# Units of 512 tokens that begin at a batch's start, and the batches' ends as a last unit

## The chip, the cores and the metric

The kernel runs on one core of a Trainium2 chip. Its time is the device time of one execution in microseconds (us), the median of three runs. The profile is one more execution with the hardware profiler on.

## The reference

Three parts follow one another. The first is attention within chunks of 64 tokens, the second a mixture of experts that sends each token to at most one expert, the third a layer with the largest of three products.

```python
# q, k, v: (8, 8, 576, 64) batch, head, token, dim; chunk = 64
scores = scale * np.matmul(q_c, k_c.transpose(0, 1, 2, 4, 3))
attn = softmax(scores)                      # within the chunk
out = np.matmul(attn, v_c)
x = out.transpose(0, 2, 1, 3).reshape(4608, 512)
do = x @ w_skip > 0                         # the rest pass unchanged
e = argmax(x @ w_gate); gate = softmax(x @ w_gate)[e]
x[do] += gate * (relu(x @ w1[e]) @ w2[e])
return max(x @ m1, x @ m2, x @ m3) @ w_out  # 768 wide, then 512
```

The chunks of 64 divide 576 evenly, and nothing in the parts after the attention depends on the order of the tokens. The weights of the third part are held in 64-bit floats.

## The kernel before

The 4608 tokens are 36 tiles of 128, in the order of batch and token. Three stages follow one another, and all of x goes through device memory (`x_dram`) between them.

**Attention and routing** (lines 124 to 683). `values`, `scores`, `exp_transpose`, `logits`, `qk_transpose` and `x_transpose` are the work of PE, and the loop at line 610 gives them their order by hand: step t takes the values of tile t-2, the scores of tile t, the turned exponentials of tile t-1, the logits of tile t-3, the turning of one job of q and k, and the turned rows of tile t-2. The order on the other engines is made by a planner from modelled times.

q and k come in 18 units (`load_qk`, line 195). Units 0 and 1 are 256 tokens with all heads, two tokens to a partition (512 B runs). Units 2 to 17 are 512 tokens with four of the eight heads, four tokens to a partition (1 KB runs), and two of them, with the same tokens, make what `item_of` numbers U (2 to 9). `pieces(t, end)` (line 182) cuts a range of tokens where a batch of 576 ends, and each piece is one load for q and one for k, on the Sync queue (line 214). The ranges of U = 2 to 8 each hold one such end: U = 2 is 64 tokens of batch 0 on 16 partitions and 448 of batch 1 on 112, the next is 32 and 96 partitions, and so on; U = 9 lies in batch 7. Units 0 and 1 lie in batch 0. That makes 66 loads of q and k.

v comes in tiles of 128 tokens (`load_v`, line 219), 256 B runs, in a ring of eight buffers; the load for tile t+6 is issued in step t. Tiles 4, 13, 22 and 31 hold a batch's end and take two loads of 64 partitions. q and k may run five units ahead of the regrouping.

POOL then copies: `cross` (line 224) puts halves of v on the other partitions, `pair_heads` (line 232) regroups q and k, and `store_x` (line 471) writes four tiles of x to `x_dram`; a tile buffer `xg` is used again two groups later. `send_id` (line 451) scatters each token's number to its expert's list, by rank. After 24 tiles the list of expert 0 is filled up to 256, so that its first two tiles can begin early. From step 22 on the weights of expert 0 are loaded and split (lines 630 to 637).

**Experts** (to line 1020): each of the eight takes its rows in tiles of 128, gathered from `x_dram`, with as many tiles as its count of rows wants, and puts them back.

**The last part** (lines 1024 to 1132): five blocks of rows of `x_dram`; its products leave through `os`, two buffers, copied in turn by VectorE and ScalarE (lines 1127 and 1129), and each tile of 128 rows is stored by one DMA (line 1131). The last block is the last 512 rows in two halves of 256, that is the last four tiles, and its four stores end the kernel.

Of the kernel before, what the change touches and what calls it, by code (L numbers as in the profile page):

```python
# [19 lines left out]
P = 128  # L20
B, H, S, D = 8, 8, 576, 64
# [7 lines left out]
NI = N // UT  # L29
WIDE = 2  # L30
NT = N // P
XW = DM + 8
COLS = NT
SLOTS = E * COLS
# [4 lines left out]
def kernel(  # L39
# [15 lines left out]
    nc = tc.nc  # L55
# [4 lines left out]
    dram = ctx.enter_context(tc.tile_pool(name="dram", bufs=1, space=DRAM))  # L60
    x_dram = dram.tile([N + 1, XW], F32, name="x_dram")
    ids_dram = dram.tile([P * SLOTS, 1], I32, name="ids_dram")
# [9 lines left out]
    def four_kb(shape, dt, name, aside=False):  # L72
        return bpool.tile(shape, dt, tag="s4" if aside else "b4", name=name, bufs=2 if aside else 4)
# [5 lines left out]
    def ps_mm(name):  # L79
        return ps(next(turns["mm"]), name)  # L80
# [8 lines left out]
    def split(src, hi, lo, eng):  # L89
        return (  # L90
            nc.scalar.copy(hi, src),  # L91
            eng.tensor_tensor(lo, src, hi.bitcast(F32), op=ALU.subtract),  # L92
        )
# [35 lines left out]
    for i in range(11):  # L129
# [6 lines left out]
        out=upper_b, in_=upper_b, compare_op=ALU.is_gt, fill=0.0, base=0,  # L136
# [4 lines left out]
    GT = 4  # L141
    SIZES = [GT] * (NT // GT - 1) + [2, 2]
    DIRECT, FIRST = NT - 4, 5
    START = [sum(SIZES[:g]) for g in range(len(SIZES))]
    PLACE = [(g, j) for g, n in enumerate(SIZES) for j in range(n)]
    prio = kpool.tile([P, GT, E], F32, name="prio")
    for e in range(E):
        nc.vector.memset(prio[:, :, e], float(E - e))
    tok_i = cpool.tile([P, NT], I32, name="tok_i")
    nc.gpsimd.iota(tok_i, pattern=[[P, NT]], base=0, channel_multiplier=1)  # L150
    tok_f = kpool.tile([P, NT], F32, name="tok_f")
    col_i = kpool.tile([P, P], I32, name="col_i")
# [23 lines left out]
    for i, t in enumerate(v_all):  # L176
        (nc.gpsimd if i > 1 else nc.vector).memset(t[:, :, D], 1.0)
    none = kpool.tile([1, XW], F32, name="none")
    nc.gpsimd.memset(none, 0.0)
    nc.gpsimd.dma_start(x_dram[N:N + 1, :], none)  # L180

    def pieces(t, end):
        got, t0 = [], t
        while t < end:
            b, s = divmod(t, S)
            n = min(end - t, S - s)
            got.append((t - t0, b, s, n))
            t += n
        return got

# [3 lines left out]
    def item_of(i):  # L194
        return (i, None) if i < WIDE else (WIDE + (i - WIDE) // 2, i % 2)

    def load_qk(i):
        if i % 5 < 3:
            qt = four_kb([P, 1024], F32, f"qt{i}", i % 5 == 2)
            kt = four_kb([P, 1024], F32, f"kt{i}", i % 5 == 2)  # L200
        else:
            both = bpool.tile([P, 2, 1024], F32, tag="b8", name=f"qkt{i}")
            qt, kt = both[:, 0], both[:, 1]
        U, g = item_of(i)
        if g is None:
            r, t0, heads = 2, i * UT, [(0, 4), (4, 8)] if i == 0 else [(0, 8)]
        else:
            r, t0, heads = 4, WIDE * UT + (U - WIDE) * 2 * UT, [(4 * g, 4 * g + 4)]
        for h0, h1 in heads:
            for off, b, s, n in pieces(t0, t0 + P * r):  # L210
                pr = slice(off // r, (off + n) // r)
                for dst, src in ((qt, q), (kt, k)):
                    to = dst[pr].rearrange("p (h x) -> p h x", x=r * D)
                    link["load"] = nc.sync.dma_start(
                        to[:, h0:h1] if g is None else to,
                        src[b, h0:h1, s:s + n, :].rearrange("h (p r) d -> p h (r d)", r=r))
        units[i] = {"qt": qt, "kt": kt}
# [86 lines left out]
    def values(t):  # L304
# [10 lines left out]
        if j == 0:  # L315
            if g == len(SIZES) - 1:
                parts = [four_kb([P, 1, XW], F32, f"xg{g}_{i}", True) for i in range(SIZES[g])]
            else:
                parts = [bpool.tile([P, GT, XW], F32, tag="xg", name=f"xg{g}")[:, :SIZES[g], :]]
            groups[g] = parts, apool.tile([P, GT, E + 1], F32, tag="lg", name=f"lg{g}")  # L320
# [147 lines left out]
    def load_ids(dst, src, eng=nc.sync):  # L468
        follow(eng.dma_start(dst, src), sent, "slots are written in any order")
# [107 lines left out]
    vm, turned, units, xt, groups, slots, picks, xgs, xT, link, put, sent = {}, {}, {}, {}, {}, {}, {}, {}, {}, {}, {}, []  # L577
# [32 lines left out]
    for t in range(NT + LAG):  # L610
        u, s = divmod(t, 2)
        while items and items[0] - 5 <= regrouped:
            load_qk(items.pop(0))
# [36 lines left out]
        if 0 <= t - 4 < NT:  # L650
            g, j = PLACE[t - 4]
            if j + 1 == SIZES[g]:
# [10 lines left out]
                if g == FIRST:  # L663
                    fill_first(run[(g + 1) % 2][:, 0, 0:1])
                    load_ids(ids_0[:, :2], ids_rows[:, :2])
                    xgs[0] = [four_kb([P, XW], F32, f"xg_0_{j}") for j in range(2)]
                    rows = START[g + 1] * P
                    at = cpool.tile([P, 2], I32, name="at")
# [131 lines left out]
    def tiles_of(rows):  # L800
        return [rows[:, j, :] for j in range(4)]

    def gather_tiles(e, js):
        if e not in xgs:
            if e < 2:
                held_rows[e] = bpool.tile([P, 4, XW], F32, tag="xg", name=f"xg_{e}")
            xgs[e] = tiles_of(held_rows[e % 2])
# [31 lines left out]
    def load_block(b, after=()):  # L839
        r0, n = BLOCKS[b]  # L840
        if b not in xin:
            tiles = [bpool.tile([P, 4, XW], F32, tag="xg", name=f"x_{b}_0")]
            if b == 0:
                tiles += [wpool.tile([P, 2, DM], F32, tag="w", name=f"x_0_{i}") for i in (1, 2)]
            elif n == G:
                tiles.append(bpool.tile([P, 4, XW], F32, tag="xg", name=f"x_{b}_1"))
            xin[b] = [t[:, i, :DM] for t in tiles for i in range(t.shape[1])]
        for i, row in enumerate(xin[b]):
            r = r0 + i * P
            follow(nc.sync.dma_start(row, x_dram[r:r + P, :DM]), after, "rows are written in any order")  # L850
# [20 lines left out]
    def ring_ahead(b, unit, by):  # L871
        while wanted and len(ring) < len(SEATS) * (b * len(UNITS) + unit) + by:
            ring_load(wpool if wanted[0][0] == LAST and len(ring) % 11 < 7 else wpool2)
# [45 lines left out]
    rows = bpool.tile([P, 4, XW], F32, tag="xg", name="xg_0")  # L919
# [165 lines left out]
    for b, (r0, n) in enumerate(BLOCKS):  # L1085
        if b < LAST:
            load_block(b + 1)
        hT = {}
        for f in range(NS):
            best = []  # L1090
            for m in range(3):
                ring_ahead(b, 3 * f + m, 8 if b < LAST else 15)
                unit(b, (m, f), best, [aside.pop(0)] if b == 0 and aside else ())
                if b == 0 and 3 * f + m >= 6:
                    for _ in range(min(2, len(rest))):
                        rest.pop(0)()
            for i in (0, 1, 3, 2):
                kf, half = 2 * f + 1 - i // 2, i % 2
                if f < 1:
                    both = four_kb([P, 2, G], F32R, f"fh_{b}_{kf}_{half}")  # L1100
                elif f < 2:
                    if i in (0, 3):
                        two = bpool.tile([P, 2, 2, G], F32R, tag="b8", name=f"fh_{b}_{kf}_{half}")
                    both = two[:, 0 if i in (0, 3) else 1]
                elif i in (0, 1):
                    both = four_kb([P, 2, G], F32R, f"fh_{b}_{kf}_{half}", True)
                else:
                    both = wpool.tile([P, 2, G], F32R, tag="w", name=f"fh_{b}_{kf}_{half}")
                hi, lo = both[:, 0, :n], both[:, 1, :n]
                split(best[i], hi, lo, nc.gpsimd)  # L1110
                hT[kf, half] = hi, lo
        if b < LAST:
            for cc in range(2):
                sums_room(b + 1, cc)
                sums_T(b + 1, cc)
            ring_ahead(b + 1, 0, 4 if b + 1 < LAST else 11)
        for half in range(2):
            for i in range(n // P):
                acc = ps_mm(f"o_{b}_{half}_{i}")
                sl = slice(i * P, (i + 1) * P)  # L1120
                for at, kf in enumerate((1, 0, 3, 2, 5, 4)):
                    hi, lo = hT[kf, half]
                    bhi, blo = mw[3, kf // 2]
                    mm3(acc, hi[:, sl], lo[:, sl], bhi[:, kf % 2, :], blo[:, kf % 2, :], at == 0, at == 5)
                o = fpool.tile([P, DM], F32, tag="o", name=f"os_{b}_{half}_{i}", bufs=2)
                if i % 2:
                    nc.scalar.copy(o, acc)
                else:
                    nc.vector.tensor_copy(o, acc)
                r = r0 + half * n + i * P  # L1130
                nc.sync.dma_start(out[r:r + P, :], o)
    p3.close()


# [28 lines left out]
```

## Time and profile before

| | |
|---|---|
| median of 3 runs | 1152.9 us (1152.66 to 1156.75) |
| the profiled execution | 1149.06 us, its span 1147.3 us |
| PE busy | 1045.2 us, 91% of the span |
| VectorE (DVE), ScalarE (ACT), POOL busy | 574.1, 440.6, 369.7 us |
| moved by DMA | 217.13 MB, 189 GB/s in the mean |
| loads and stores on the hardware queue of Sync (q1) | 183680 packets, 174.18 MB |

A busy PE is one with matmuls in flight, not one at its peak. The DMA share is the mean busy share of 16 DMA engines; a packet counts from its start to its end, so that packets in flight together can bring it above 1. "issue" as a reason for a wait is time in which the engine waited for nothing that the profile shows. A wait for several things is put down to the one that came last.

### The profile page before, as it was taken

What the parts mean: (1) busy time and instruction counts of PE and PEld (TensorE: products, weight loads), DVE (VectorE), ACT (ScalarE), POOL (GpSimd) and SP (SyncE); (2) the same over time, 40 slices, a digit from 0 to 9 for tenths busy, and PEclk for the clock granted to TensorE, in tenths of its full rate; (3) what the DMA queues carried; (4) which work ended last, traced back from release to release, by engine and by line L of the source; (5) the groups of instructions that cost most, each with busy time, mean ns of one, the idle gap of its engine ahead of it and who ended that gap; (6) DMA issues with size and microseconds to landing.
All of it is one profiled execution on the core that took longest, in us unless ns stands there. A gap on an engine that the chain in (4) does not pass through costs nothing.

```text
span 1147.3 us, 19676 instructions
## 1 busy us (share of the span) xinstructions
PE 1045.2 (91%) x7544; PEld 887.4 (77%) x7544; DVE 574.1 (50%) x1118; ACT 440.6 (38%) x737; POOL 369.7 (32%) x411
## 2 busy tenths in 40 slices
PE   7777877887989997999799799999999999999997
PEld 6667767785877877888678678878887888778896
DVE  4545555657784728643359882344423451334241
ACT  5645666423443424442234343222322232222231
POOL 3444465336432415432233323121401231122121
PEclk9978888778989999999999989999999999999999
DMA  9999955237675637742789854665456645666591
GB/s 208 204 225 185 234 141 162 94 114 241 202 281 193 180 117 258 241 170 82 251 273 308 275 167 157 192 188 170 156 149 190 189 131 159 185 187 197 179 299 37
DMA packets 196977, 217.13 MB, mean 189 GB/s; under 512 B 48523, under 2 KB 161163, under 8 KB 196864
## 3 DMA queue, kind: packets, MB, share of 16 engines
q1 hardware_dynamic: 183680, 174.18, 53.6%
q0 software_dynamic: 10592, 33.20, 8.4%
q10 hardware_dynamic: 2592, 8.26, 1.9%
q8 instruction: 69, 1.13, 0.4%
q14 instruction: 44, 0.36, 0.1%
HBM read 175.15 MB, written 41.83 MB: 189 GB/s over the span
## 4 chain that ended last, share of the span: by engine, by line
PE 39%; DMA 6%; DVE 3%; issue 3%; POOL 1%; ACT 0%; SPq 0%; POOLq 0%; DVEq 0%; ACTq 0%
PE f_a L720 5%; PE f_a L722 5%; PE f_a L721 5%; PE o L720 4%; PE o L722 4%; PE o L721 4%; DMA ws<-m_sums 3%; PE f_d L720 3%; PE f_d L722 2%; PE f_d L721 2%; DMA m_sums<-n_q 2%; PE f_b L722 1%; PE f_b L720 1%; PE f_b L721 1%; PE trf L894 1%
## 5 line engine op out<-in xcount | busy, mean ns | idle before, releaser
L92 POOL TENSOR_TENSOR fh<-best,fh 128x512 fp32r<-128x512 f32 (+1 forms) x60 | 77.4, 1295 | 360.5 <-ACT fh L91 275.5
L720 PE MATMUL f_a<-x_t,ws 128*128 128x512 f32 (+1 forms) x270 | 100.9, 374 | 6.0 <-DVE p L1048 5.2
L721 PE MATMUL f_a<-x_t,ws 128*128 128x512 f32 (+1 forms) x270 | 99.9, 370 | 0.0
L722 PE MATMUL f_a<-x_t,ws 128*128 128x512 f32 (+1 forms) x270 | 99.8, 370 | 0.0
L91 ACT CAST whi_e<-raw_e 128x1024 fp32r<-128x1024 f32 x64 | 65.9, 1048 | 62.3 <-DMA raw_e<-in_moe_w_dram 28.5
L720 PE MATMUL h<-xhi,whi_e 128*128 128x256 f32 x256 | 75.3, 295 | 13.3 <-ACTq L997 7.6
L721 PE MATMUL o<-wlo_m,fh 128*128 128x512 f32 x216 | 84.6, 392 | 0.0
L720 PE MATMUL o<-whi_m,fh 128*128 128x512 f32 x216 | 83.4, 392 | 0.0
L722 PE MATMUL o<-whi_m,fh 128*128 128x512 f32 x216 | 83.4, 392 | 0.0
L722 PE MATMUL y<-whi_e,hlo 128*128 128x512 f32 x184 | 73.3, 402 | 3.5 <-DVE hlo L727 3.3
L720 PE MATMUL y<-whi_e,hhi 128*128 128x512 f32 x184 | 74.0, 404 | 0.6 <-ACT hhi L787 0.6
L721 PE MATMUL h<-xlo,whi_e 128*128 128x256 f32 x256 | 74.2, 290 | 0.0
L722 PE MATMUL h<-xhi,wlo_e 128*128 128x256 f32 x256 | 74.0, 290 | 0.0
L721 PE MATMUL y<-wlo_e,hhi 128*128 128x512 f32 x184 | 72.7, 397 | 0.0
L92 DVE TENSOR_TENSOR wlo_e<-raw_e,whi_e 128x1024 fp32r<-128x1024 f32 x43 | 58.5, 1375 | 24.6 <-ACT whi_e L91 21.9
L92 POOL TENSOR_TENSOR wlo_e<-raw_e,whi_e 128x1024 fp32r<-128x1024 f32 x21 | 53.2, 2537 | 51.3 <-ACT whi_e L91 51.1
L91 ACT CAST fh<-best 128x512 fp32r<-128x512 f32 (+1 forms) x60 | 34.7, 579 | 89.6 <-DVE best L1050 57.6
L720 PEld LDWEIGHTS h<-xhi,whi_e 128*128 128x128 f32 x256 | 51.1, 200 | 16.2 <-ACTq L997 8.0
L720 PEld LDWEIGHTS f_a<-x_t,ws 128*128 128x128 f32 x270 | 51.2, 189 | 15.7 <-DVE p L1048 5.7
L1053 ACT COPY p<-f_a 128x512 f32<-128x512 f32 (+1 forms) x45 | 24.5, 544 | 100.5 <-PE f_a L722 100.3
L711 POOL DMA_INDIRECT x_dram<-xg,ids_sb x20 | 21.9, 1096 | 118.5 <-DVEq L935 46.8
L722 PEld LDWEIGHTS f_a<-x_t,ws 128*128 128x128 f32 x270 | 51.2, 190 | 8.7
(220 smaller groups left out, 2759.9 us busy)
## 6 DMA issues: line engine op xcount, KB each, us to landing
ws<-m_sums SPq DMA_DIRECT2D x135, 512.0 KB
raw_e<-in_moe_w_dram SPq DMA_DIRECT2D x64, 512.0 KB
ws<-m_sums SPq DMA_DIRECT2D x45, 256.0 KB
x<-x_dram SPq DMA_DIRECT2D x36, 256.0 KB
out_dram<-os SPq DMA_DIRECT2D x36, 256.0 KB
x_dram<-xg POOLq DMA_DIRECT2D x8, 1040.0 KB
v_all<-in_v_dram SPq DMA_DIRECT2D x32, 256.0 KB
m_sums<-n_raw ACTq DMA_DIRECT2D x18, 448.0 KB
```

The source lines that it names most:

```text
L91: nc.scalar.copy(hi, src),
L92: eng.tensor_tensor(lo, src, hi.bitcast(F32), op=ALU.subtract),
L711: ins = nc.gpsimd.indirect_dma_start(out=x_dram[:, :], out_offset=bass.IndirectOffsetOnAxis(ap=ids, axis=0), in_=xg, in_offset=None, bound ...
L720: nc.tensor.matmul(acc, ahi, bhi, start=first, stop=False, skip_group_check=onto)
L721: nc.tensor.matmul(acc, ahi, blo, start=False, stop=False, skip_group_check=onto)
L722: return nc.tensor.matmul(acc, alo, bhi, start=False, stop=last, skip_group_check=onto)
L894: nc.tensor.transpose(tr[:, i * P:(i + 1) * P], row[:, c * P:(c + 1) * P], ident)
L1053: nc.scalar.copy(p1, acc_a)
```

## The change

The first 512 tokens of the eight batches are put first, batch by batch (4096 tokens, 32 tiles), and the last 64 of each follow as the last 512 (4 tiles). `pieces` returns the parts of a range in that order. So the units U = 2 to 8 are batches 1 to 7, one piece over 128 partitions each, and tiles 0 to 31 of v are one load each. U = 9 is the ends of all batches: its q and k are loaded head by head, eight batches to a load, 16 partitions for each batch, 16 loads in all. Tiles 32 to 35 hold two batches' ends each, so v takes two loads for each. At the end, rows that belong to those tiles are stored by two DMAs of 64 rows to the places of their batches; other tiles by one. `x_dram` and the lists of the experts hold the tokens in the new order. Nothing else changes.

```diff
--- before.py
+++ after.py
@@ -29,6 +29,9 @@
 NI = N // UT
 WIDE = 2
 NT = N // P
+WHOLE = S // P * P
+TAIL = S - WHOLE
+FULL = B * WHOLE // P
 XW = DM + 8
 COLS = NT
 SLOTS = E * COLS
@@ -182,9 +185,9 @@
     def pieces(t, end):
         got, t0 = [], t
         while t < end:
-            b, s = divmod(t, S)
-            n = min(end - t, S - s)
-            got.append((t - t0, b, s, n))
+            b, s = divmod(t, WHOLE) if t < P * FULL else divmod(t - P * FULL, TAIL)
+            n = min(end - t, (WHOLE if t < P * FULL else TAIL) - s)
+            got.append((t - t0, b, s if t < P * FULL else s + WHOLE, n))
             t += n
         return got
 
@@ -206,7 +209,14 @@
             r, t0, heads = 2, i * UT, [(0, 4), (4, 8)] if i == 0 else [(0, 8)]
         else:
             r, t0, heads = 4, WIDE * UT + (U - WIDE) * 2 * UT, [(4 * g, 4 * g + 4)]
-        for h0, h1 in heads:
+        if t0 >= P * FULL:
+            b0, nb = (t0 - P * FULL) // TAIL, P * r // TAIL
+            for h in range(heads[0][0], heads[0][1]):
+                for dst, src in ((qt, q), (kt, k)):
+                    link["load"] = nc.sync.dma_start(
+                        dst.rearrange("p (h x) -> p h x", x=r * D)[:, h - heads[0][0], :],
+                        src[b0:b0 + nb, h, WHOLE:, :].rearrange("b (p r) d -> b p (r d)", r=r))
+        for h0, h1 in heads if t0 < P * FULL else ():
             for off, b, s, n in pieces(t0, t0 + P * r):
                 pr = slice(off // r, (off + n) // r)
                 for dst, src in ((qt, q), (kt, k)):
@@ -1128,7 +1138,9 @@
                 else:
                     nc.vector.tensor_copy(o, acc)
                 r = r0 + half * n + i * P
-                nc.sync.dma_start(out[r:r + P, :], o)
+                for off, b_out, s_out, rows in pieces(r, r + P):
+                    at = b_out * S + s_out
+                    nc.sync.dma_start(out[at:at + rows, :], o[off:off + rows])
     p3.close()
```

## Rows read from the trace of the kernel before

**Rows 1.** Page, part 2: PE, its granted clock, DMA, GB/s in 40 slices.

```profile
PE   7777877887989997999799799999999999999997
PEclk9978888778989999999999989999999999999999
DMA  9999955237675637742789854665456645666591
GB/s 208 204 225 185 234 141 162 94 114 241 202 281 193 180 117 258 241 170 82 251 273 308 275 167 157 192 188 170 156 149 190 189 131 159 185 187 197 179 299 37
```

**Rows 2.** Windows of four tiles: length, busy us (instructions) by engine, clock, DMA share, GB/s.

```profile
20.30:42.40 22.10, 18.33 (x372) 15.67 (x367) 9.37 (x20) 16.89 (x26) 8.54 (x18) 1.00 1.08 205
42.40:66.80 24.40, 18.41 (x356) 16.72 (x357) 13.78 (x43) 16.03 (x27) 8.79 (x18) 0.93 1.18 224
66.80:95.20 28.40, 21.11 (x355) 19.15 (x355) 12.98 (x42) 14.83 (x25) 12.78 (x23) 0.76 1.21 225
95.20:121.00 25.80, 19.52 (x360) 17.71 (x359) 12.88 (x43) 14.55 (x25) 12.68 (x23) 0.87 0.94 186
121.00:148.40 27.40, 22.38 (x351) 19.76 (x350) 12.55 (x42) 15.01 (x26) 17.29 (x28) 0.79 0.84 196
148.40:170.60 22.20, 19.59 (x356) 17.34 (x356) 14.69 (x43) 14.56 (x25) 13.66 (x23) 0.87 0.48 145
170.60:196.80 26.20, 21.20 (x355) 18.67 (x355) 15.76 (x50) 15.40 (x27) 17.39 (x28) 0.80 0.54 168
196.80:221.70 24.90, 20.34 (x338) 17.95 (x338) 14.89 (x44) 14.76 (x26) 10.81 (x19) 0.74 0.31 104
```

**Rows 3.** Windows by kind of load, same columns.

```profile
4.00:10.00 6.00, 4.69 (x26) 3.13 (x28) 0.98 (x2) 3.40 (x6) 1.24 (x4) 1.00 1.01 288
...
64.00:88.00 24.00, 16.71 (x266) 15.46 (x262) 10.69 (x37) 10.06 (x18) 13.35 (x23) 0.72 1.21 210
...
132.00:143.00 11.00, 10.92 (x186) 10.23 (x185) 5.93 (x16) 7.35 (x13) 5.77 (x13) 0.77 1.10 327
```

**Rows 4.** Waits of PE, 42.4 to 148.4 us: total, times, longest.

```profile
PE sc L278 <- issue: 12.4, 18, 3.0
PE trq L262 <- POOL qr L239: 5.7, 2, 3.5
...
PE xp L311 <- issue: 1.4, 1, 1.4
```

**Rows 5.** Waits of PE, 148.4 to 221.7 us.

```profile
PE sc L278 <- issue: 1.6, 3, 0.9
```

**Rows 6.** Waits of POOL, 42.4 to 148.4 us.

```profile
POOL xg L322 <- DMA x_dram<-xg: 26.9, 4, 7.6
POOL vm L230 <- DMA ids_dram<-tok_i,rslot: 12.5, 3, 6.3
```

**Rows 7.** Waits of POOL, 148.4 to 221.7 us.

```profile
POOL xg L322 <- DMA x_dram<-xg: 10.2, 3, 4.1
```

**Rows 8.** Timeline of PE: start, length, idle before in brackets, its releaser.

```profile
36.33 0.66 PE L262 MATMUL trk<-ident,kr 128*128 128x128 f32 x4 [1.14 <-POOL kr L239]
...
49.90 0.29 PE L278 MATMUL sc<-kT,qT 64*64 64x64 f32 x4 [2.95 <-issue]
...
65.77 0.27 PE L311 MATMUL xp<-vm,aT 64*64 64x65 f32 x1 [1.36 <-issue]
...
80.46 1.11 PE L262 MATMUL trq<-ident,qr 128*128 128x128 f32 x4 [3.54 <-POOL qr L239]
...
148.60 0.26 PE L278 MATMUL sc<-kT,qT 64*64 64x64 f32 x1 [0.94 <-issue]
```

**Rows 9.** Tile qt, issues on the Sync queue: ns least/median/most, first and last start.

```profile
L214 SPq DMA_DIRECT2D qt<-in_q_dram x21: 390/663/3767, 0.8 to 134.4; - x21
```

**Rows 10.** Chain that ended last, 1135 us to the end: start, length.

```profile
1140.48 0.34 SPq L1131
...
1140.91 2.28 DMA out_dram<-os
```

## Prediction

> **What bounds the kernel now.** I read the page's slices first. The DMA line stands at 9 for the first five slices (some 143 us) while TensorE (PE) is at 7 or 8 and the granted clock falls below full from the third slice on [rows 1]. This is the attention stage, 36 tiles of 128 tokens, and the only stage whose loads the change touches; the expert stage and the last stage do the same work on the same number of rows afterwards.
>
> So I cut that stage into windows of four tiles, from one normalising multiply (line 326) to the fourth after it [rows 2]. Nothing is steadily full: PE is busy for about three quarters of each window, with its order fixed by hand, so a tile's time is set by whichever helper comes late. The windows between 42.4 and 148.4 us take 24.4, 28.4, 25.8 and 27.4 us, 106.0 together, with a DMA share of 0.84 to 1.21. The next three take 22.2, 26.2 and 24.9 us, 73.3 together, with a share of 0.31 to 0.54. I treat these as the same work with and without busy DMA, though the later ones also cast expert 0's weights (lines 630 to 637).
>
> Then I asked whether the loads or the amount of data make DMA busy [rows 3]. At 4 to 10 us every load covers 128 partitions, in 512 B packets: 288 GB/s at a share of 1.01. At 132 to 143 us the last unit's loads, again 128 partitions and 1 KB packets, run beside v and the store of x: 327 GB/s at 1.10. In between, where a 512-token unit straddles a batch's end and comes as two pieces (16 and 112 partitions, 32 and 96, ...), the same share and more (1.21 at 64 to 88 us) moves 210 GB/s. The engines are as busy and deliver a third less.
>
> Last, I asked who pays. PE waited 12.4 us at the scores and 1.4 at the values for "issue", that is for nothing a semaphore shows, and 5.7 us for GpSimd (POOL) regrouping q: 19.5 us in the four windows [rows 4]. In the three later ones the "issue" wait at the scores is 1.6 us [rows 5]. POOL itself waited 26.9 us for stores of x and 12.5 us before copies of v halves [rows 6]; the second is put down to the id scatter, but the copies that follow it read v, and v loads queue behind q and k, so I read it as late v. In the later windows the store wait is 10.2 us [rows 7]. The longest single gaps are 3.54 us at 80.46 for POOL and 2.95 us at 49.90 for "issue" [rows 8]. [...]
>
> **The change, part by part.** *q and k.* The packets do not change: they were 1 KB and stay 1 KB, and bytes are equal. What goes is the cut. Seven of the eight 512-token units lose it, so the 66 q and k loads become 50 (6 for batch 0, 28 for batches 1 to 7, 16 for the ends). The 28.3 MB of q, k and v take 28.3/0.21 = 135 us at the rate of the cut loads and 87 to 98 us at 327 or 288 GB/s. The windows of [rows 2], 32 of the 36 tiles, reach to 221.7 us, so DMA goes from the thing that is late to a thing with room. What that is worth I bound from both sides by [rows 2]: if the four congested windows run like the mean of the three later ones (24.4 us), they take 97.7 and the gain is 8.3 us; if like the best one (22.2), 88.8 and 17.2 us. The waits agree with the lower end: 19.5 us of PE waits become about 4/3 of 1.6, but the later windows have other waits in their place. I take 12 us, near the middle, since the later windows carry those casts and the earlier ones don't.
>
> *The first tiles.* Up to 42.4 us two heads' groups are turned per step and ScalarE is busy for 16.9 of 22.1 us [rows 2]; the only PE wait here behind a load is 1.14 us at 36.33, for POOL's copy of k [rows 8]. I take 1 us; the bounds are 0 and 3.
>
> *v.* 40 loads before and after. Four split tiles become whole and the last four are split instead, with the same two pieces of 64 partitions; their time is inside the rates above. Cost nothing on their own: tile t's load is issued six steps ahead, some 6 x 6 = 36 us of cover.
>
> *The batches' ends.* Unit 9 now takes 16 loads of 128 KB instead of 4 of 512 KB. They go through the Sync queue, with v loads behind them. One issue takes 0.39 us unhindered, 0.66 in the median and 3.77 at most [rows 9]; 16 are 6 to 11 us, against a lead of 36 us of v and more for q and k. I count them as hidden. [...]
>
> [...]
>
> *The order of tokens.* Rows of x now stand in another order, and routing places them by rank. Worked out from the reference's inputs, each expert's total is the same; expert 0 has 182 instead of 184 rows in the first 24 tiles, which are padded to 256 either way, and 93 instead of 91 after, still one tile. No branch changes. Zero.
>
> *Outputs.* The last block's four stores become eight, of 64 rows. At the end two copies wait for the buffers of two earlier stores: store issue 0.34 us, landing 2.28 us [rows 10]. Each buffer's second store is issued 0.34 us later; the second buffer's comes fourth instead of second, and the last tile has one more issue behind it. That is 0.34 x 2 for the wait and 0.34 for the last store, 1.0 us; if half-size stores land earlier, 0.4. I take +0.9. Elsewhere the store is unchanged.
>
> **The sum.** -12 - 1 + 0.9 = -12.1 us. The profiled execution took 1149.06 us, 1.8 around its span; it would take 1137. The median of the runs is 1152.9, 3.8 above it; taken off there: 1140.8, which I put at 1141. By the bounds: 1133 to 1146. A measurement of this kernel can tell about 0.5%, 5.8 us, from no change.
>
> **Rivals.** *Less comes off.* The "issue" waits may need only a burst of loads, not slow ones. For: around 145 us, right after loads at 327 GB/s, PE still waited, the last time 0.94 us at 148.60 [rows 3, 8]. Against: after 148.4 they nearly vanish [rows 5]. Then only POOL's waits go: 5.7 + 1 - 0.9 = 5.8 us, 1147; if new waits on ScalarE and VectorE fill part of it, up to 1152. Chance 0.21.
>
> *More comes off.* [...] The window at 42.4 has clock 0.93 and took 24.4 us with 2.95 and 1.36 us of gaps in it [rows 2, 8]; without them 20.1, four times 80.4, a gain of 25.6 us: 1127. Against: the window with the least DMA, share 0.31, still took 24.9 at clock 0.74. Chance 0.13.
>
> *Slower: the 16 end loads block the Sync queue.* If each issue takes as long as the longest before (3.77 us) [rows 9], 16 take 60 us, v is 60 - 36 = 24 us late for the tiles behind, and the whole comes to 1141 + 24 = 1165. It costs from 36/16 = 2.3 us an issue, and makes the kernel slower than before from about 3 us. [...] Against: an issue that nothing hinders takes 0.39, and half of all take 0.66 or less, in a queue that the cut loads kept full [rows 9]. Chance 0.06; another 0.03 goes to the order that the planner writes for the other engines from its new load times, which could open a few gaps like the longest seen, 3.54 us each [rows 8], or close as many.
>
> **How the numbers follow.** The forecast, 1133 to 1146, has 0.57. The range of 8 in 10 leaves out half of "more" and the slower cases: 1128 to 1153. Faster by over 0.5% (below 1147.1): 0.57 + 0.13 + a small part of "less", 0.72. Within 0.5%: 0.20. Slower: 0.08.
>
> **What would show it.** Right: in the profile after, the stretch that loads whole units runs near 290 GB/s or above at a share near 1, the DMA line falls under 9 before the fifth slice, POOL's waits for stores and v halve, tile 20's multiply comes some 13 us before 148.4, and the expert stage starts by as much earlier. The stores at the end are eight, and the last copy waits about 0.7 us longer. Wrong: if the DMA rate rises and tile 20 does not move, the pace is that of the hand-written order and its helpers; if the rate stays near 210, the cut was not the cause; if tiles 28 to 35 wait for v or POOL for q at unit 9, the end loads are.

## The result and the profile after

The changed kernel takes 1138.5 us in the median of four runs (1136.2 to 1140.7), the kernel before 1152.8 beside it (1149.2 to 1156.8). The ratio is 0.9875, its 95% interval 0.9837 to 0.9913: 14 us faster. The profiled executions are 1149.06 and 1138.35 us, 10.7 apart, so the rows below can account for 10.7 of the 14. In what follows one kernel (new order, cut as before) had three slower runs among its twelve, 1158 to 1160 us, which its median includes and its ratio leaves out.

First the loads. The page after, part 2, answers [rows 1] (PE, its granted clock, DMA, GB/s in 40 slices):

```profile
PE   7888887897899997999899799999999999999996
...
PEclk8979788688999998999999899999999999999999
DMA  9985645237574828651899835665456645666581
GB/s 247 309 224 151 188 123 177 103 122 253 185 285 142 266 75 276 212 179 59 268 324 312 262 126 184 189 180 155 165 161 184 193 139 149 185 186 207 189 271 37
```

DMA stood at 9 for five slices and now stands there for two; the second slice moves 309 GB/s instead of 204. Windows of the changed kernel, by kind of load, beside [rows 3] (length, busy us by engine, clock, DMA share, GB/s):

```profile
24.00:36.00 12.00, 10.41 (x212) 8.95 (x216) 4.73 (x10) 10.05 (x17) 5.75 (x12) 1.00 1.05 273
40.00:60.00 20.00, 16.10 (x338) 13.59 (x337) 11.20 (x40) 12.91 (x22) 9.87 (x16) 1.00 1.13 326
64.00:88.00 24.00, 20.98 (x353) 18.81 (x353) 13.27 (x42) 13.20 (x24) 14.77 (x26) 0.79 0.66 181
114.00:116.00 2.00, 2.00 (x11) 2.00 (x12) 1.32 (x8) 1.20 (x4) 1.90 (x4) 0.50 0.51 140
```

Whole units move 273 to 326 GB/s where the cut ones moved 210 at a higher share, and from 64 us on the share is 0.66: the loads have caught up with the kernel. The last row lies among the loads of the batches' ends. A store of x (1.07 of 6.52 MB) is part of the 326, so the queue of the loads is read by itself: packets, MB and the share that its packets took, at 40 to 60 us, in the kernel before and in the changed one.

```profile
q1 hardware_dynamic: 5718, 3.84, 118.2%
```

```profile
q1 hardware_dynamic: 8545, 5.38, 97.3%
```

That is 192 and 269 GB/s, and the larger amount took less packet time.

Then the pace. Windows from one normalising multiply (line 336 now) to the fourth after it, tiles 4 to 32, beside [rows 2]:

```profile
41.30:66.10 24.80, 20.41 (x354) 17.60 (x353) 12.56 (x43) 15.21 (x27) 9.90 (x17) 0.89 1.06 291
66.10:89.80 23.70, 20.61 (x367) 18.47 (x360) 13.29 (x43) 13.56 (x24) 15.56 (x28) 0.83 0.68 184
89.80:111.50 21.70, 18.16 (x354) 15.74 (x355) 13.01 (x43) 15.28 (x27) 9.64 (x17) 0.93 0.66 192
111.50:138.60 27.10, 23.42 (x367) 21.48 (x360) 13.56 (x42) 15.59 (x27) 14.77 (x27) 0.75 0.60 168
138.60:162.70 24.10, 21.60 (x366) 19.63 (x358) 14.14 (x43) 15.60 (x26) 14.60 (x25) 0.78 0.46 134
162.70:188.70 26.00, 20.67 (x367) 17.87 (x359) 14.75 (x50) 14.79 (x26) 13.47 (x22) 0.83 0.56 170
188.70:213.10 24.40, 21.13 (x350) 18.32 (x342) 14.87 (x45) 14.33 (x26) 10.85 (x17) 0.71 0.30 105
```

The first four are the congested ones: 24.8 + 23.7 + 21.7 + 27.1 = 97.3 us instead of 106.0. PE was busy for 82.6 us of them, and for 81.4 before: what went is PE's idle time, 14.7 us instead of 24.6. So the pair of profiles differs by -1.1 us before tile 4, -8.7 in tiles 4 to 20, +1.1 from there to tile 35 (94.0 before, 95.1 after), -4.1 from tile 35 to the last matmul (897.3 and 893.2, the same work), and +2.2 behind it: -10.6 of 10.7. How far single executions of these stretches differ is shown below.

Waits of PE and of POOL in 41.3 to 138.6 us, beside [rows 4] and [rows 6] (total, times, longest; `sc` are the scores, `lp` the logits, `xg` a tile's rows of x, `vm` the copied halves of v):

```profile
PE sc L288 <- issue: 4.1, 11, 0.5
PE lp L357 <- ACT xt L351: 3.6, 6, 0.7
PE sc L288 <- ACT kT L274: 3.0, 4, 0.8
...
POOL xg L332 <- DMA x_dram<-xg: 20.3, 4, 5.8
POOL vm L240 <- DMA ids_dram<-tok_i,rslot: 11.1, 3, 5.1
```

PE's wait for POOL's copies of q (5.7) is gone, and "issue" at the scores is down from 12.4 to 4.1; POOL's two waits are somewhat shorter (26.9 and 12.5 before). One more wait of POOL, for v itself, stood in the kernel before (42.4 to 148.4 us) and has no row now:

```profile
POOL vm L230 <- DMA v_all<-in_v_dram: 4.6, 1, 4.6
```

The end, in the chain that ended last, beside [rows 10] (start, length):

```profile
1126.63 0.24 PE o L732
...
1127.61 0.54 SPq L1143
...
1128.20 0.59 SPq L1143
...
1128.90 0.53 SPq L1143
...
1129.48 2.36 DMA out_dram<-os
...
1131.94 0.59 ACT os L1137
```

Three issues of half stores stand in a row, 0.53 to 0.59 us each where a whole store took 0.34, and the copy waits for the landing of the third.

### The profile page after: what moved, and what is told of

Read it like the earlier page. It is cut to its first block, busy times and chain, and to the rows that moved or that the text cites. A ratio compares the mean times of both kernels' runs of the same rounds, so it can differ in the third digit from the quotient of the medians.

```text
span 1136.6 us, 19653 instructions
## 1 busy us (share of the span) xinstructions
PE 1044.0 (92%) x7544; PEld 885.6 (78%) x7544; DVE 572.4 (50%) x1118; ACT 441.3 (39%) x737; POOL 370.3 (33%) x411
## 4 chain that ended last, share of the span: by engine, by line
PE 40%; DMA 5%; DVE 3%; issue 2%; POOL 1%; ACT 0%; SPq 0%; DVEq 0%; POOLq 0%; ACTq 0%
PE f_a L730 5%; PE f_a L732 5%; PE f_a L731 5%; PE o L730 4%; PE o L732 4%; PE o L731 4%; DMA ws<-m_sums 3%; PE f_d L730 3%; PE f_d L732 2%; PE f_d L731 2%; DMA m_sums<-n_q 2%; PE f_b L730 1%; PE f_b L732 1%; PE f_b L731 1%; PE trf L904 1%
## 5 line engine op out<-in xcount | busy, mean ns | idle before, releaser
L95 DVE TENSOR_TENSOR wlo_e<-raw_e,whi_e 128x1024 fp32r<-128x1024 f32 x43 | 56.2, 1322 | 24.3 <-ACT whi_e L94 19.8
L1063 ACT COPY p<-f_a 128x512 f32<-128x512 f32 (+1 forms) x45 | 24.6, 546 | 95.4 <-PE f_a L732 95.2
L721 POOL DMA_INDIRECT x_dram<-xg,ids_sb x20 | 21.7, 1087 | 117.5 <-DVEq L945 46.9
```

The costliest lines, as they stand in the source:

```text
L721: ins = nc.gpsimd.indirect_dma_start(out=x_dram[:, :], out_offset=bass.IndirectOffsetOnAxis(ap=ids, axis=0), in_=xg, in_offset=None, bound ...
L1063: nc.scalar.copy(p1, acc_a)
```

## The experiments

All ratios are to the kernel before, run on the same chip; its median there was 1147.3 us for the first four kernels, 1149.6 for the next four, 1146.2 for the last four.

| kernel | median us | ratio (95%) |
|---|---|---|
| two loads of two heads | 1127.2 | 0.9824 (0.9790 to 0.9857) |
| new order, cut as before | 1153.3 | 1.0036 (1.0007 to 1.0066) |
| unit 9 as whole loads | 1140.2 | 0.9921 (0.9894 to 0.9949) |
| no loads behind the first | 1198.2 | not to be compared |
| always cut 16 and 112 | 1148.3 | 1.0010 (0.9973 to 1.0047) |
| padding on VectorE | 1136.0 | 0.9875 (0.9822 to 0.9927) |
| logits' copy first | 1133.5 | 0.9853 (0.9799 to 0.9906) |
| four output buffers | 1138.5 | 0.9892 (0.9822 to 0.9961) |
| the change again | 1130.4 | 0.9861 (0.9836 to 0.9887) |
| padding on VectorE and logits' copy first | 1112.5 | 0.9697 (0.9672 to 0.9722) |
| two loads, four buffers | 1118.7 | 0.9767 (0.9735 to 0.9798) |
| two loads, four buffers, padding on VectorE | 1114.6 | 0.9728 (0.9699 to 0.9756) |

**Is it the cut by partitions, or the number of loads?** Two kernels issue 78 loads of q and k instead of 50, one by heads and one by partitions. By heads:

```diff
+            if t0 < P * FULL:
+                heads = [(4 * g, 4 * g + 2), (4 * g + 2, 4 * g + 4)]
...
-                        to[:, h0:h1] if g is None else to,
+                        to[:, h0:h1] if g is None else to[:, h0 - 4 * g:h1 - 4 * g],
```

> The changed kernel with each whole unit loaded by two loads of two heads, both over 128 partitions: 78 loads of q and k instead of 50, no partition left out of any of them. Theory P (a load that covers only some partitions slows the stream): the rate at 40 to 60 us stays near the 326 GB/s of the changed kernel, and the time within 3 us of its 1138.5. Rival N (it is the number of loads, their issues and their waits): with more loads than the 66 of before the gain is gone, 1149 to 1155, and the rate falls towards 195 GB/s.

By partitions, in the new order of tokens, at the place where the kernel before cut:

```diff
-            for off, b, s, n in pieces(t0, t0 + P * r):
+            whole = pieces(t0, t0 + P * r)
+            if g is not None:
+                c, (off, b, s, n) = TAIL * (U - 1), whole[0]
+                whole = [(0, b, s, c), (c, b, s + c, n - c)]
+            for off, b, s, n in whole:
```

> The changed kernel, new order of tokens and ends as they are, with each whole unit of q and k cut in two by partitions where the kernel before cut it (16 and 112, 32 and 96, up to 112 and 16): 78 loads again. Theory P: the rate at 40 to 60 us falls to 190 to 230 GB/s and the time goes back by most of the gain, to 1147 to 1154. Rival N: the same time as the cut by heads, which has the same number of loads. Rival O (the order of tokens or the planner's new order of instructions made the gain): stays at 1138.5, whatever the rate does.

And the same cut always at partition 16 (`c` is `TAIL`), so that seven eighths of the bytes go by loads of 112 partitions:

> The change with the new order of tokens, but each whole unit's tensor as two loads, always of its first 16 and its last 112 partitions (78 issues on the Sync queue). If what costs is that a load starts away from partition 0 or covers a small part of the partitions, the stretch of whole units runs near 200 GB/s at a share above 1.1, as in the kernel whose cut moved by 16 from unit to unit, and the time is 1147 to 1157 us. If only the loads of the odd cuts in the middle are slow and a load of 112 partitions runs as one of 128, the rate is 270 or more and the time is that of the change, 1136 to 1142 us.

The stretch of whole units in the kernel cut by heads, and in the one always cut at 16 (same columns as above):

```profile
40.00:60.00 20.00, 17.00 (x354) 14.89 (x350) 12.69 (x42) 14.66 (x26) 9.12 (x14) 1.00 1.06 302
```

```profile
40.00:60.00 20.00, 17.38 (x360) 15.34 (x359) 13.27 (x43) 15.37 (x28) 8.88 (x17) 1.00 1.16 219
```

With as many loads, those over all partitions move 302 GB/s, and the kernel is no slower than the change (1127.2 us where the expectation had 1138.5 within 3; the intervals 0.9790 to 0.9857 and 0.9837 to 0.9913 overlap). Those cut by partitions move 219 at a higher share, and the whole gain is gone (1.0010 and 1.0036). In the kernel always cut at 16 the queue of the loads (40 to 60 us) and the waits of PE and of POOL (41.9 to 140.7 us) are again near those of the kernel before:

```profile
q1 hardware_dynamic: 6548, 4.14, 111.8%
```

```profile
PE trq L276 <- POOL qr L253: 6.1, 3, 3.7
...
POOL xg L336 <- DMA x_dram<-xg: 27.9, 4, 7.6
...
POOL vm L244 <- DMA v_all<-in_v_dram: 4.6, 2, 3.3
```

The planner's order of the small work is not what separates these kernels either. Up to tile 35 VectorE and ScalarE run the same instructions in the same order in the kernel before, in the change and in both kernels cut by partitions; GpSimd's order is the same in the change and in the kernel cut as before, and elsewhere differs by neighbours that change places in two or three spots. Number and size of the loads, the order of the tokens and the planner's order are thus not what the change pays for; the cut by partitions is. The cut at 16 is enough for it, though its large pieces cover 112 partitions. Where in the stage the time is lost is less clear: in the profile of the kernel cut at 16, tiles 4 to 20 take 98.8 us, hardly more than in the change's, and tiles 20 to 35 take 104.6.

Cut at 16, the queue of the loads moves 207 GB/s in the mean (4.14 MB in 20 us), and 269 with whole loads. Whether the loads of 112 partitions are slow themselves, or only those of 16 between them, is not shown; these views don't tell their packets apart.

**Do the 16 loads of the batches' ends cost?** Unit 9 as four whole loads, which read batch 7's tokens once more:

```diff
         if t0 >= P * FULL:
+            t0 = P * FULL - P * r
+        if False:
```

> The changed kernel with unit 9, the ends of the batches, loaded by 4 whole loads of 512 KB over 128 partitions from the tokens of batch 7 instead of 16 loads of 128 KB; it computes on the wrong tokens there. Theory: the 16 loads are hidden behind the lead of q, k and v, so the time stays within 3 us of 1138.5, while the Sync queue is free 8 to 12 us earlier around 125 us. Rival: the end loads cost what group 111 to 139 us lost (27.1 us against 21.7 to 24.8 of the others), 3 to 5 us, and the time falls to 1134.

1140.2 us at 0.9921: no faster than the change, though 512 rows hold other values here and can route otherwise. The 16 issues in the changed kernel (least, median and most ns, first and last start) are

```profile
L216 SPq DMA_DIRECT2D qt<-in_q_dram x8: 598/650/1648, 112.4 to 128.1; - x8
L216 SPq DMA_DIRECT2D kt<-in_k_dram x8: 598/605/1419, 114.7 to 128.8; - x8
```

At most 1.65 us, and not the 3.77 us of the rival; they cost nothing that can be seen.

At 114 to 116 us these loads move 140 GB/s at a share of 0.51. How many of the 16 engines they used is not shown: a mean share does not tell which engines were idle.

**What is left for the loads to cost?** Nothing is loaded after unit 4 of q and k and after tile 7 of v:

```diff
     def load_qk(i):
+        if i > 4:
+            units[i] = {nm: units[2 + i % 3][nm] for nm in ("qt", "kt")}
+            return
...
     def load_v(t):
+        if t >= NV:
+            return
```

> The changed kernel without the loads of q and k after unit 4 and of v after tile 7 (later tiles compute on the earlier ones' data): what the attention stage takes when these loads can neither be late nor disturb anything. Theory H (after the change the stage runs at the pace of its hand-written order and its helpers): tiles 4 to 20 take 90 to 96 us against 97.3, the whole 1130 to 1138. Rival D (it still pays for loads, by waits for instructions and for POOL): tiles 4 to 20 take 76 to 86 us, the whole 1112 to 1126.

Other rows of x route otherwise, and with 969 us behind tile 35 instead of 903 the whole can't be compared. The attention stage can be read: tiles 4 to 20 take 94.0 us, 3.3 less than the change's 97.3. Their window, and below it waits of PE and of POOL at 41 to 135 us in this kernel:

```profile
41.50:135.50 94.00, 77.94 (x1417) 69.56 (x1416) 50.24 (x169) 59.12 (x102) 51.10 (x88) 0.90 0.13 48
```

```profile
PE sc L293 <- issue: 7.5, 15, 1.1
...
POOL xg L337 <- DMA x_dram<-xg: 14.1, 4, 3.9
...
POOL vm L245 <- DMA ids_dram<-tok_i,rslot: 1.9, 1, 1.9
```

PE is idle for 16.1 us here (94.00 less 77.94) and for 14.7 in the change: its loads of q, k and v leave no idle time of PE in this stage that these two profiles show. The lengths themselves say less, since single profiles spread by more than 3.3 us, as will be seen (85.9 in the kernel that loads by heads). And the "issue" wait is there without loads, larger than in the change: it is no measure of what loads cost. What does shrink is POOL's wait behind the id scatter, from 11.1 to 1.9. What sets the pace of the stage now is asked next.

**The order of the small work.** The kernel with two loads of two heads differs from the change in more than its loads. The planner wrote another order: on ScalarE the copy of a tile's logits stands ahead of the next exponentials in most of the first tiles, and on POOL the zeroing of x's padding, which waits for a store of x, comes later. Its POOL waits 4.3 us for stores in tiles 4 to 20 instead of 20.3. Each of the two was laid on the change alone. The padding:

```diff
-            for part in parts:
-                nc.gpsimd.memset(part[:, :, DM + 1:], 0.0)
...
-        nc.vector.tensor_tensor(
+        done = nc.vector.tensor_tensor(
...
+        if j == 0:
+            for part in groups[g][0]:
+                with tc.issue_after(done.ins):
+                    nc.vector.memset(part[:, :, DM + 1:], 0.0)
```

> The change, with the zeroing of the padding columns of the x rows moved from GpSimd to VectorE, right behind the multiply that writes the first tile of the group. In the change GpSimd stands 20.3 us in four waits for the store of x that frees these rows, ahead of its copies of v, q and k. Theory that these waits open TensorE's gaps (and with them the stretches at the lower clock): the wait goes, tiles 4 to 20 take 86 to 92 us instead of 97.3, the whole 1127 to 1133 us. Rival, that the load shape of the kernel with two loads of two heads is what made it faster: no change, 97 us and 1136 to 1141 us. Rival on the other side: VectorE's multiply meets the store itself and TensorE waits for it: over 100 us and above 1142 us.

The copy of the logits (`link["lg"]`); the block of expert 0's weights keeps its place behind the exponentials:

```diff
-        link["exp"] = nc.scalar.activation(ex, ex, AF.Exp, scale=D ** -0.5)
...
+        if t < NT:
+            with tc.issue_after(link["lg"].ins) if "lg" in link else nullcontext():
+                ex = units[u]["ex", s]
+                link["exp"] = nc.scalar.activation(ex, ex, AF.Exp, scale=D ** -0.5)
```

> The change, with the copy of the logits of tile t-3 on ScalarE always ahead of the exponentials of tile t, as the planner placed it in the kernel with two loads of two heads, and behind them in nearly every tile of the change. Theory that this order is what made that kernel faster: tiles 4 to 20 in 86 to 90 us, the whole 1127 to 1132 us. Rival, that its loads or GpSimd's order made it: tiles 4 to 20 stay at 97 us, the whole 1136 to 1141 us; or worse, up to 1146 us, where the exponentials wait for the logits on TensorE.

Neither theory came true. The first edit gives 0.9875, the second 0.9853, with tiles 4 to 20 at 94.2 and 96.4 us: by their intervals neither can be told from the change. Then both together, on one chip with the change itself:

> The change itself, beside the kernels it is to be compared with, on one chip. Its ratio to the kernel before should repeat .9875 [.9837, .9913].

> The change with its own loads (one of 512 KB per unit and tensor), and with both orders of the kernel with two loads of two heads laid on it: the copy of the logits ahead of the exponentials on ScalarE, and the zeroing of the padding off GpSimd. Each alone left tiles 4 to 20 at 94 to 96 us. If the order of the small work is all that made that kernel faster, tiles 4 to 20 take 86 to 89 us and the whole 1127 to 1131 us. If the loads' halves do it, by letting the first pair of heads start on half the data, tiles 4 to 20 stay at 92 to 97 us and the whole at 1132 to 1138 us.

Together they give 1112.5 us against the change's 1130.4, 17.9 us less, and 0.9697 of the kernel before, with the change's own loads. It is the lowest median of all, below both ranges of the expectation. That the order of the small work pays is shown by this; which wait pays is read from single profiles. Windows of the change in this second execution (tiles 4 to 20, tiles 20 to 35):

```profile
40.90:122.10 81.20, 69.94 (x1419) 62.21 (x1420) 51.05 (x169) 59.10 (x102) 42.22 (x76) 0.96 0.80 228
122.10:222.60 100.50, 76.25 (x1229) 68.16 (x1228) 58.33 (x190) 53.29 (x94) 48.05 (x78) 0.73 0.50 147
```

and of the kernel with both orders:

```profile
41.10:122.40 81.30, 71.55 (x1418) 64.86 (x1418) 53.98 (x173) 59.42 (x102) 48.40 (x81) 0.92 0.89 247
122.40:205.00 82.60, 65.98 (x1228) 58.25 (x1229) 57.87 (x196) 53.81 (x94) 42.04 (x64) 0.85 0.50 157
```

and, as a third, of the kernel with four output buffers (below), which is the change up to its last stage:

```profile
40.90:139.40 98.50, 83.04 (x1419) 73.29 (x1419) 52.67 (x170) 59.63 (x102) 51.29 (x89) 0.84 0.74 208
139.40:232.80 93.40, 74.50 (x1241) 65.68 (x1239) 56.23 (x189) 53.01 (x94) 41.58 (x66) 0.80 0.44 138
```

The same instructions, in the same order on each engine, thus took 97.3, 81.2 and 98.5 us for tiles 4 to 20. Most of that is PE's busy time at another granted clock: 82.6 and 83.0 us at 0.84, 69.9 at 0.96; its idle time was 14.7, 11.3 and 15.5. Over tiles 4 to 35 the change took 192.4, 181.7 and 191.9 us, and the kernel with both orders 163.9, less than any of the three.

Against the execution beside it the difference lies in tiles 20 to 35, 100.5 and 82.6, 17.9 us, of which 3.6 are lost again behind tile 35: these two executions are 14.0 apart. Against the other two it lies in both stretches. What opens the gap in the second execution can be followed in the change's POOL (start, length, and in brackets the idle time before and its releaser):

```profile
115.04 0.85 POOL L240 COPY vm<-v_all 64x260 f32<-64x260 f32 x2
121.84 0.12 POOL L332 MEMSET xg<- 128x28 f32 x1 [5.96 <-DMA x_dram<-xg]
...
127.14 0.97 POOL L463 DMA_INDIRECT ids_dram<-tok_i,rslot  x1 [0.31 <-issue]
132.96 0.84 POOL L240 COPY vm<-v_all 64x260 f32<-64x260 f32 x2 [4.84 <-DMA ids_dram<-tok_i,rslot]
133.86 0.61 POOL L249 COPY qr<-qkt 128x512 f32<-128x512 f32 x1
```

and in its PE:

```profile
134.53 1.11 PE L272 MATMUL trq<-ident,qr 128*128 128x128 f32 x4 [5.48 <-POOL qr L249]
```

A memset of 0.12 us holds POOL for 5.96 us, since it waits for the store of x that frees its buffer; the scatters behind it are late, the copy of v waits 4.84 us behind those, the copy of q comes after that, and PE stands 5.48 us for it. In the first execution the same memset waited 5.79 us and the same copy 4.66, but PE, at a clock of 0.75 there, was later than POOL and had no such gap: what it gains before tile 20 it can lose here. In the kernel with both orders no wait for a store of x is left in POOL, and none of PE for POOL, from 122.4 to 205 us; POOL still waits 4.8 us behind the id scatter. The granted clock differs too, 0.73 in the mean against 0.85. One gap of 5.48 us is a part of the 17.9; how much of the rest the stores' waits and how much ScalarE's order gives, these profiles don't separate.

Two more kernels went with these: the two loads of two heads with four buffers for the output rows, and the same with the padding on VectorE.

> Each whole unit and tensor as two loads of two heads over all 128 partitions, and four buffers for the rows of the output. The first took tiles 4 to 20 to 85.9 us from 97.3, the second the end behind the last matmul to 8.2 us from 9.7. Together 1138.5 - 11 - 1.5 = about 1126 us, and 1123 to 1130 us; if the gain of the two loads was one chip's or one run's, 1133 to 1138 us, within 3 us of the change beside it.

> The kernel with two loads of two heads and four output buffers, with the zeroing of the padding on VectorE too. That kernel kept one wait of 4.3 us of GpSimd for a store of x in tiles 4 to 20, and has three more behind them. If GpSimd's waits still cost, 2 to 4 us under the kernel without the move, 1121 to 1125 us; if they don't, equal within 2 us; if the planner's order that the two loads brought is lost by the move, 1130 to 1136 us.

1118.7 and 1114.6 us, the first below the range that was expected. The two loads with their order thus gain about 10 us over the change on the same chip (11.7, less 1.5 for the buffers, next paragraph). The moved padding gives about 4 more, and its interval (0.9699 to 0.9756) overlaps that of the kernel without it (0.9735 to 0.9798) and that of whole loads with both orders (0.9672 to 0.9722). Whether the two loads gain by their halves' earlier landing or by the order that came with them stays open; both orders on whole loads do at least as much without the halves.

**The end.** Four buffers for the rows of the output instead of two:

```diff
-                o = fpool.tile([P, DM], F32, tag="o", name=f"os_{b}_{half}_{i}", bufs=2)
+                o = fpool.tile([P, DM], F32, tag="o", name=f"os_{b}_{half}_{i}", bufs=4)
```

> The change, with four buffers instead of two for the rows of the output, so that no copy at the end waits for a store. After the change the last matmul is 9.7 us from the end, 7.6 before. If the wait of the last copies for the buffers of the stores (now two stores per half tile) makes the end longer, it falls to 6 to 8 us and the whole to 1135 to 1137 us; if the Sync queue's issues of .53 to .59 us each set it, the end stays within 0.5 us of 9.7.

Its chain of waits, at the end:

```profile
1127.60 0.24 PE o L732
...
1127.89 0.43 issue
1128.33 0.61 ACTq L1170
```

No copy waits for a landing any more, and the span ends at 1136.0, 8.2 us behind the last matmul instead of 9.7 (1126.87 to 1136.6). The two effects share it: 1.5 us for the buffers; the other 0.6 over the 7.6 of before I lay to the longer issues of half stores (0.53 to 0.59 us each in the change's chain, 0.34 before), an estimate. In the median (1138.5, where 1135 to 1137 was expected) 1.5 us can't be told from none.

## Why the prediction was right, and where not

The forecast was 1141 with 1128 to 1153; 1138.5 came. By its steps:

- *The cause.* Right, and shown: the cut by partitions slowed the stream. Put back in the new order it takes the gain away, 1.0010 and 1.0036; more loads without it do not. The DMA rate of whole units (273 to 326 GB/s) and the DMA line did what the prediction wrote. The rows it was inferred from were weaker than they look: 1.07 of the 3.59 MB at 132 to 143 us before are a store of x, and the loads alone moved 2.51 MB there (228 GB/s) against 4.88 MB at 64 to 88 us (203). What tells them apart is the packet time, a share of 77.3% against 118.4%.
- *-12 us for tiles 4 to 20.* The bounds of 8.3 and 17.2 held the 8.7 of the profile, near the lower end; I had taken the middle. But one profile of each kernel is not enough for a term of this size: the change itself took 97.3 us in one execution and 81.2 in another, where the later tiles took 100.5 instead of 95.1. The steadier part is PE's idle time in these tiles, 24.6 us before and 14.7, 11.3 and 15.5 in three executions of the change; the rest, PE's busy time, was 81.4 us at a granted clock of 0.83 before and 82.6, 69.9 and 83.0 at 0.84, 0.96 and 0.84, and the term did not count the clock. The other two executions would have given 24.8 and 7.5, both outside the bounds, so that this profile's 8.7 lies inside them is luck. The reliable sizes are those of the medians, -14.3 and -15.8 us.
- *Who pays.* Half wrong. PE's wait for POOL's q (5.7) went as written in tiles 4 to 20; in the second execution one of 5.48 us stands at tile 22, behind POOL's stores. The "issue" waits I laid to the loads; the kernel without loads has 7.5 us of them. And POOL's wait at the copies of v, which the view put down to the id scatter, I read as late v and expected to halve; it went from 12.5 to 11.1. In the second profile of the change the copy at 132.96 is of tile 22, whose load was issued by 98.6, long before. The view was right, though the wait does hang on loads: without them it is 1.9. Late v was another row, 4.6 us once, and that went.
- *POOL's wait for stores.* I expected half of 26.9; it is 20.3, and 14.1 without loads. Most of it is in the order of the work, and the fastest kernel takes it away.
- *-1 us up to tile 4.* 1.1.
- *End loads, order of tokens, v at nothing.* Held by the runs with unit 9 as whole loads and with the old cut in the new order. The longest issue is not 3.77 us, which is that of `qt` alone; one of `kt` took 4.52 before. Those of the end loads took at most 1.65. Tile 20's multiply came 9.8 us earlier, tile 35's 8.7.
- *+0.9 us at the end.* 2.2. The step that failed is the issue of a half store at 0.34 us: it takes 0.53 to 0.59, and three stand in a row.
- *The rivals.* "Less" would have kept POOL's 5.7 us as the only gain; more came. "More" took two gaps out of the window at 42.4 us and wrote four times the rest, 80.4 us, for tiles 4 to 20. The second execution of the change came to that, 81.2 us at 0.96, and lost 6.5 us of it in tiles 20 to 35 (100.5 us where the kernel before took 94.0), where POOL's waits stand; its median gained 15.8 us, not 25.6. "Slower" asked for 3 us an issue; they take 0.60 to 0.65 in the median. To a new order of the planner I had given a chance of 0.03: the order hardly changed with the change. What the order costs in the change I had not asked, and it is the largest thing found here that is left.
- Not foreseen: 4.1 us less between tile 35 and the last matmul, in the same work. With 895.9 and 895.0 us in the second execution and in the kernel with four output buffers, against 893.2 and 897.3 before, most of it is the spread of single executions.

## What to carry to other kernels

Read GB/s beside the DMA share, for the queue of the loads alone: a share as high at some 30% less of the rate (118.2% at 192 GB/s, 97.3% at 269 after) was here the mark of loads of poor shape, and cutting them so that each covers all partitions was worth more than having fewer (0.9824 with 78 loads over all partitions, 1.0010 and 1.0036 with 78 cut by partitions). When loads stop being late, read next who stands ahead of others on its engine: here a memset of 0.12 us waited 5.96 us for a store and held the copies behind it. Moving it alone gave nothing that could be told from noise, and moving it together with one ScalarE copy gave about as much again as the change (17.9 and 15.8 us). Before a term of 10 us is read from the windows of one profile, read a second execution, and split each window into PE's busy and idle time.

## What the runs showed of the hardware

- Whole loads of q and k, each cut into one of the first 16 and one of the other 112 partitions, brought the queue of the loads of q, k and v from 5.38 to 4.14 MB in 20 us (269 to 207 GB/s, 40 to 60 us), while the share that its packets took rose from 97.3% to 111.8%: the engines look no less busy.
- The eight stores of 64 rows at the end took 0.47 to 0.59 us each to issue, the four of 128 rows in the same place before 0.33 to 0.38; the landing that a copy waited for was no shorter (2.36 us, 2.28 before).
- PE's waits for "issue" came in the middle of one tile's scores, 0.19 to 0.50 us at a time, in three bursts in tiles 4 to 20 of the change (at 56 to 59, 84 to 86 and 127 to 131 us), with and without loads (4.1 us at the scores there, 7.5 without loads), and less in the second execution of the change (1.1 us in 40 to 140 us). What ends them the profile doesn't show, and no run here settled it.
- The same instructions took 97.3, 81.2 and 98.5 us for tiles 4 to 20 in three executions, with a granted clock of 0.84, 0.96 and 0.84.
